# Sums and weighted values of eight heads in one burst: hash-masked attention and a maxout FFN on one core

## The chip, the core and the metric

The kernel runs on one core of one Trainium2 chip. It uses five instruction queues: TensorE (PE, with its weight loads listed as PEld), VectorE (DVE), ScalarE (ACT), GpSimd (POOL) and SyncE (SP, which only issues transfers); POOL and ACT issue transfers too. The metric is the device time of one execution in microseconds (us). Three runs of the kernel before took 264.42, 264.56 and 264.79 us; the median is 264.56 us. The times of the profile were taken on one further execution, of 264.41 us, whose span from the first to the last instruction is 262.4 us.

## The reference: what is computed

Attention over 4 batches, 8 heads, 768 positions and a head size of 64, in which a query sees only keys of the same hash bucket (six sign bits of a projection), and then, over the rows with the heads side by side, a maximum of three products and an output product:

```python
q_bits = (einsum('bhsd,dk->bhsk', q, proj) > 0)      # six bits, likewise k_bits
mask = q_bucket[:, :, :, None] == k_bucket[:, :, None, :]
scores = where(mask, scale * q @ k.T, -1e9)
attn = exp(scores - max); attn = attn / (attn.sum(-1) + 1e-9)
x = (attn @ v)  -> rows of batch and position, columns of head and size: 3072 x 512
out = maximum(maximum(x @ w1, x @ w2), x @ w3) @ w_out     # 512 -> 768 -> 512
```

## The kernel before, in words

The order of all instructions is written out by hand: each engine executes its own instructions in program order, and the program is one loop over 192 **units** (L613). The queries of a batch are cut into **chunks**: batch 0 into three chunks of 256 queries (chunks 0 to 2), batches 1 to 3 into two of 384 each (chunks 3 to 8). A unit is a part of one chunk and one head: 768 scores in each of 128 partitions. The hash bits are appended as six or eight further rows to q and k, so that one matmul gives the masked score.

**A unit.** `scores(u)` (L282) issues two or three PE matmuls (L298) into one of two PSUM buffers `sc`, takes a free SBUF tile `AT` from a list of 24 in order of release, and lets ACT write the exponentials into it (L306). The scores of unit u+1 are issued at the start of turn u. An `AT` tile holds its blocks with two columns of ones behind each; its blocks are 256 or 384 wide, and when a tile is taken in the other width the two columns are written anew, by DVE in `scores` (L304), or by POOL when the tile is given back (L395, for the second half of the heads of batch 0). From chunk 3 on DVE adds the parts of one head together (`add`, L322, two turns behind the unit), and from chunk 5 on also the two halves of that sum.

**A burst** (`burst`, L341) serves one chunk and four heads. It runs one turn behind the last of these heads' units in batch 0, and four turns behind later. Its `sums` is a set of matmuls with 32 columns of ones per head (L358), four heads side by side in one PSUM bank; DVE transposes the bank in blocks of 32 (L365), adds a small constant and takes the reciprocal of one column per block (L367, L368), and spreads it back by a transpose into `rb` (L369). Its `values`, twice, is 24 matmuls with 32 columns each (L380) and one DVE operation into `xT` (L387), which multiplies by `rb`. Then the `AT` tiles of the four heads are given back. Chunks 3 to 8 have their bursts at turns 63, 75, 87, and so on every 12 turns, up to 183 and one after the last turn.

**The FFN** (`ffn_groups`, L402) of a chunk is a list of groups: 18 groups of four matmuls (L413; six column blocks times three weights), whose first product of three is copied from PSUM to `ht` and whose second and third are taken into it by a DVE maximum (L422); then two output groups of three matmuls (L457) for every 128 rows, an ACT copy into a buffer `osb` (L461) and a store from SP (L463). One such group is issued per turn up to turn 47 and 1.15 per turn after that, so that chunk 0's six first products are issued at turns 34 to 39, chunk 1's FFN lasts from turn 55 to 74, chunk 2's to 93, and each later one about 21 turns. The first product is copied by ACT where the chunk is 384 wide (L418) and by DVE in batch 0 (L420).

Sums, values, hash and FFN groups share four PSUM banks, taken and given back in rotation (`bank`, L90).

**Later sets.** q and k of batches 1 to 3 come as "sets" of four heads. They are loaded into `nat` buffers, turned by DVE in four transposes of 32-blocks (L202), narrowed by POOL (L207), and placed by SP transfers into `S` (L212). `quad_hash` (L214) is 16 fp32 matmuls (L221), a DVE comparison into `bits` (L224) and four SP transfers (L232) one turn later. Their turns are written out in the set-up ahead of the loop: the four transposes of a set of batch 2 are spread over nine turns from turn 61 on, of batch 3 over twelve from turn 100 on; a set is placed three turns behind its last transpose; the hash of sets 4, 5, 6 and 7 is issued at turns 84, 99, 135 and 147.

Of the kernel before, what the change touches and what calls it, by code (L numbers as in the profile page):

```python
# [17 lines left out]
def kernel(  # L18
# [31 lines left out]
    RS = 2.0 ** -5  # L50
    SCALE = 0.125 / (RS * RS)
    EPS = 2.0 ** -60
    NAT = 24
    SPREAD = {2: (61, 9), 3: (100, 12)}
    THIRD_ADD = 5
    LAG = (1, 4)
    ATW = 776

    konst = ctx.enter_context(tc.tile_pool(name="konst", bufs=1))
    nat_pool = ctx.enter_context(tc.tile_pool(name="nat", bufs=6))  # L60
    t32_pool = ctx.enter_context(tc.tile_pool(name="t32", bufs=3))
    t16_pool = ctx.enter_context(tc.tile_pool(name="t16", bufs=3))
    s_pool = ctx.enter_context(tc.tile_pool(name="spool", bufs=6))
    b_pool = ctx.enter_context(tc.tile_pool(name="bpool", bufs=2))
    vo_pool = ctx.enter_context(tc.tile_pool(name="vopool", bufs=4))
    small = ctx.enter_context(tc.tile_pool(name="small", bufs=4))
    ad_pool = ctx.enter_context(tc.tile_pool(name="adpool", bufs=5))
    ys_pool = ctx.enter_context(tc.tile_pool(name="yspool", bufs=2))
    rb_pool = ctx.enter_context(tc.tile_pool(name="rbpool", bufs=2))
    x_pool = ctx.enter_context(tc.tile_pool(name="xpool", bufs=3))  # L70
    h_pool = ctx.enter_context(tc.tile_pool(name="hpool", bufs=8))
    o_pool = ctx.enter_context(tc.tile_pool(name="opool", bufs=2))
    sc_ps = ctx.enter_context(tc.tile_pool(name="sc_ps", bufs=2, space=bass.MemoryType.PSUM))
    ms_ps = ctx.enter_context(tc.tile_pool(name="ms_ps", bufs=1, space=bass.MemoryType.PSUM))

# [2 lines left out]
    pj2 = konst.tile([P, Q], FP32, name="pj2")  # L78
    pst = konst.tile([Q, 2, NBITS], FP32, name="pst")
    ones = konst.tile([P, Q], FP16, name="ones")  # L80
    at_tiles = [konst.tile([P, ATW], FP16, name=f"AT{i}", tag=f"AT{i}") for i in range(NAT)]
    warm = h_pool.tile([P, HALF], FP16, tag="ht", name="warm")
    w_sb = [konst.tile([P, NJC, DF], FP16, name=f"w{i}_sb", tag=f"w{i}_sb") for i in range(3)]
# [22 lines left out]
    def s_tile(name):  # L106
        if name not in s_of:
            s_of[name] = s_pool.tile([D + KB, 4, S], BF16, tag="S", name="S")
        return s_of[name]
# [104 lines left out]
    def quad_hash(g):  # L214
        i, bp = bank()
        ts = [t32.pop((side, g)) for side in range(2)]
        for u in range(2):
            for side in range(2):
                for j in range(2):
                    r = 2 * side + j  # L220
                    nc.tensor.matmul(bp[Q * r : Q * (r + 1), 0:HALF], pj[:, u, :],  # L221
                                     ts[side][:, u, j * HALF : (j + 1) * HALF], start=(u == 0), stop=(u == 1))
        bits = b_pool.tile([P, HALF], BF16, tag="bits", name="bits")
        nc.vector.tensor_scalar(out=bits[:], in0=bp[:, 0:HALF], scalar1=0.0, scalar2=0.5,  # L224
                                op0=AluOp.is_gt, op1=AluOp.subtract)
        give(i)

        def send():
            for side in (1, 0):
                for j in range(2):  # L230
                    r = 2 * side + j
                    nc.sync.dma_start(s_of[side, g][D : D + KB, :, j * HALF : (j + 1) * HALF],  # L232
                                      bits[Q * r : Q * (r + 1), :])
        return send

# [105 lines left out]
    def burst(c, i):  # L341
        b, q0, w = chunks[c]
        held = {}
        rb = []

        def own_bank(key):
            if c == NCH - 1 and i == 1 and key != 1:
                return None, sc_ps.tile([P, 2, 512], FP32, tag="sc", name="sc")[:, 0, :]
            return bank()

        def sums(m0, m1):
            if m0 == 0:
                held["s"] = own_bank("s")
            sm = held["s"][1]
            bs = [sum_blocks(c, 4 * i + x) for x in range(4)]
            for m in range(len(bs[0])):
                for x in range(4):
                    nc.tensor.matmul(sm[Q * x : Q * (x + 1), 0:w], ones[:, :], bs[x][m],  # L358
                                     start=(m == 0), stop=(m == len(bs[0]) - 1))
            if m1 == NM:  # L360
                ys = ys_pool.tile([P, HALF], FP32, tag="ys", name="ys")
                rr = small.tile([P, HALF // Q], FP32, tag="rr", name="rr")
                n = w // Q
                rb.append(rb_pool.tile([P, HALF], FP32, tag="rb", name="rb"))
                nc.vector.transpose(ys[:, 0:w], sm[:, 0:w])  # L365
                give(held["s"][0])
                nc.vector.tensor_scalar(out=rr[:, 0:n], in0=ys[:, 0:w:Q], scalar1=EPS * S, scalar2=None, op0=AluOp.add)  # L367
                nc.vector.reciprocal(rr[:, 0:n], rr[:, 0:n])  # L368
                nc.vector.transpose(rb[0][:, 0:w], rr[:, 0:n].unsqueeze(2).to_broadcast((P, n, Q)))  # L369

        def values(side, m0, m1):
            if m0 == 0:
                held[side] = own_bank(side)
            av = held[side][1]
            first = (b, i, side) not in sv_of
            n = w + 1 if first else w
            for m in range(m0, m1):
                cb = block_of(b, m)
                for x in range(4):
                    nc.tensor.matmul(av[Q * x : Q * (x + 1), 0:n], v_at[2 * b + i][:, x, cb * D + side : (cb + 1) * D : 2],  # L380
                                     weights_of(c, 4 * i + x, m)[:, 0:n], start=(m == 0), stop=(m == NM - 1))
            if m1 == NM:
                if first:
                    sv_of[b, i, side] = small.tile([P, 1], FP32, tag=f"sv{side}", name="sv")
                    nc.vector.tensor_scalar(out=sv_of[b, i, side][:], in0=av[:, w : w + 1], scalar1=EPS, scalar2=None,
                                            op0=AluOp.mult)
                nc.vector.scalar_tensor_tensor(out=xt_of(c)[:, 2 * i + side, 0:w], in0=av[:, 0:w],  # L387
                                               scalar=sv_of[b, i, side][:], in1=rb[0][:, 0:w], op0=AluOp.add, op1=AluOp.mult)
                give(held[side][0])
                if side == 1:  # L390
                    for h in range(4 * i, 4 * i + 4):
                        for n in range(parts_of(c)):
                            a = at_of[unit_at[c, h, n]]
                            if b == 0 and i == 1:
                                nc.gpsimd.memset(blocks(at_tiles[a], HALF)[:, :, HALF : HALF + 2], 1.0)  # L395
                                at_form[a] = HALF
                            at_free.append(a)

        return sums, values


    def ffn_groups(c):  # L402
# [6 lines left out]
        for fb, wi in jobs:  # L409
            def go(fb=fb, wi=wi):  # L410
                k_, ps = bank()
                for jc in range(NJC):
                    nc.tensor.matmul(ps[:, 0:w], w_sb[wi][:, jc, fb * P : (fb + 1) * P], xt[:, jc, 0:w],  # L413
                                     start=(jc == 0), stop=(jc == NJC - 1))
                if wi == 0:
                    hts[fb] = h_pool.tile([P, HALF], FP16, tag="ht", name="ht")
                    if w == HALF:
                        nc.scalar.copy(hts[fb][:, 0:w], ps[:, 0:w])  # L418
                    else:
                        nc.vector.tensor_copy(hts[fb][:, 0:w], ps[:, 0:w])  # L420
                else:
                    nc.vector.tensor_tensor(out=hts[fb][:, 0:w], in0=hts[fb][:, 0:w], in1=ps[:, 0:w], op=AluOp.max)  # L422
                give(k_)
            gs.append(go)
# [54 lines left out]
    def when(u, f, *args):  # L479
        at.setdefault(u, []).append(lambda: f(*args))  # L480

    with tc.manual_schedule():
# [10 lines left out]
        load_quad(1, 2, range(4), nc.sync)  # L493
        nc.vector.memset(pj2[:], 0.0)
        nc.vector.memset(ones[:], 1.0)
        for t in at_tiles:
            nc.vector.memset(blocks(t, THIRD)[:, :, THIRD : THIRD + 2], 1.0)
        for hd in range(2):
# [76 lines left out]
        for g in range(2, NQUAD):  # L575
            b2, i2 = divmod(g, 2)
            need = UPB * b2 + 12 * i2
            for n, side in enumerate((1, 0)):
# [7 lines left out]
                for n2, u2 in enumerate(us):  # L586
                    when(u2, turn, name, n2 // 2, n2 % 2)
                    if n2 % 2:
                        when(u2 + 1, narrow, name, n2 // 2)
                when(us[3] + 3, place, name, range(4))  # L590
            hash_at[{2: 32, 3: 47, 4: need - 12}.get(g, need - 9)] = g
            when({2: 36, 3: 46}.get(g, need - 22), load_v, g)

        ffn, credit = [], 0
# [1 line left out]
        last_of = {}  # L596
        for c, i in sorted(done_at, key=lambda e: done_at[e]):
            d = done_at[c, i] + LAG[c > 2]
            sums, values = burst(c, i)
            pieces = [lambda f=sums: f(0, NM), lambda f=values: f(0, 0, NM), lambda f=values: f(1, 0, NM)]  # L600
            for n, f in enumerate(pieces):
                u = {(0, 0): (16, 17, 20), (1, 0): (21, 22, 24), (2, 0): (26, 27, 29)}.get((c, i), (d, d, d))[n]
                todo.setdefault(u, []).append(f)
            last_of[c] = max(u, last_of.get(c, 0))
# [65 lines left out]
```

## Time and profile before

| what | value |
|---|---|
| median of three runs | 264.56 us |
| profiled execution | 264.41 us |
| its span | 262.4 us |
| PE busy | 256.5 us (98%) |
| DVE busy | 207.8 us (79%) |
| ACT busy | 177.9 us (68%) |
| POOL busy | 69.8 us (27%) |
| granted TensorE clock | 1.00 throughout |
| DVE busy from 75 to 111 us | 34.72 of 36 us |
| ACT busy from 60 to 75 us | 12.54 of 15 us |

How to read it: a group of instructions is given by line, engine, operation, tiles and count, then its busy time, the mean duration of one, and the idle time of its engine just before it with what ended that. In the timeline, neighbouring instructions of one kind are merged: start, length from the first start to the last end, engine, line, tiles, count. Matmuls overlap: the next one starts long before the one ahead has ended, and so the distance from start to start tells how long PE is taken, and a duration does not. The same holds to a smaller degree for ACT and DVE, whose next instruction starts up to 0.11 us ahead of the recorded end of the last.

### The profile page before, as it was taken

The numbers are of one execution on the slowest core, as the hardware profiler recorded it, in microseconds if no ns is written. First come the engines' busy times: TensorE is split into PE (matmuls) and PEld (weight loads), VectorE is DVE, ScalarE is ACT, GpSimd is POOL, SyncE is SP. The second block draws the span as 40 slices with busy tenths as digits, with TensorE's granted clock in tenths as the row PEclk, the third lists the DMA queues.
The fourth block names the chain that finished last, engine by engine and source line by source line (L and its number), as shares of the span: only waits on it lengthen the run. The fifth ranks groups of instructions, "written<-read, shape, count | busy, mean of one in ns | idle before, by whom it ended". The sixth has DMA issues, their size and how long they took to land.

```text
span 262.4 us, 6477 instructions
## 1 busy us (share of the span) xinstructions
PE 256.5 (98%) x2503; PEld 154.4 (59%) x2503; DVE 207.8 (79%) x492; ACT 177.9 (68%) x258; POOL 69.8 (27%) x132
## 2 busy tenths in 40 slices
PE   8999999999999999999999999999999999999995
PEld 4655658865765666555555554655555555555552
DVE  2897767966799999969999996899849795888350
ACT  3797886667968675956869588584886859581322
POOL 3878752355043526330141612011000000000000
PEclk9999999999999999999999999999999999999999
DMA  6998999979732964970073653802030003000303
GB/s 210 326 224 170 170 235 226 217 132 204 187 91 75 202 139 61 273 186 17 0 198 104 116 127 49 210 0 58 20 122 1 0 2 121 2 0 2 120 0 120
DMA packets 20717, 30.95 MB, mean 118 GB/s; under 512 B 2608, under 2 KB 15248, under 8 KB 20688
## 3 DMA queue, kind: packets, MB, share of 16 engines
q0 software_dynamic: 8128, 13.37, 27.3%
q1 hardware_dynamic: 12128, 16.66, 22.0%
q10 hardware_dynamic: 432, 0.52, 0.6%
q8 instruction: 19, 0.31, 0.5%
q14 instruction: 10, 0.08, 0.1%
HBM read 25.17 MB, written 6.29 MB: 120 GB/s over the span
## 4 chain that ended last, share of the span: by engine, by line
PE 89%; DVE 5%; ACT 3%; issue 2%; DVEq 0%; ACTq 0%
PE ms L413 34%; PE sc L298 22%; PE ms L457 11%; PE ms L380 10%; PE ms L221 3%; ACT AT L306 3%; PE ms L358 3%; PE ms L171 1%; PE ms L123 1%; PE ms L504 1%; DVE ht L422 1%; DVE ad L329 1%; DVE xT L387 1%; PE ms L150 1%; PE ms L438 1%
## 5 line engine op out<-in xcount | busy, mean ns | idle before, releaser
L306 ACT ACTIVATE AT<-sc 128x768 f16<-128x768 f32 x192 | 152.4, 816 | 57.2 <-PE sc L298 53.9
L413 PE MATMUL ms<-xT,w_sb 128*128 128x384 f16 (+1 forms) x648 | 115.0, 307 | 0.3 <-DVE xT L387 0.2
L298 PE MATMUL sc<-S 72*128 72x384 bf16 (+1 forms) x432 | 93.8, 308 | 1.2 <-ACT AT L306 0.9
L413 PEld LDWEIGHTS <-w_sb 128*128 128x128 f16 x648 | 62.7, 97 | 35.9 <-issue 0.4
L422 DVE TENSOR_TENSOR ht<-ht,ms 128x384 f16<-128x384 f16 (+1 forms) x108 | 54.2, 503 | 20.7 <-PE ms L413 10.5
L298 PEld LDWEIGHTS <-S 72*128 72x128 bf16 (+1 forms) x432 | 39.4, 98 | 31.8 <-issue 11.8
L207 POOL TENSOR_SCALAR T<-T 128x768 bf16<-128x768 f32 x24 | 22.8, 951 | 90.2 <-issue 48.4
L457 PE MATMUL ms<-wout_sb,ht 128*128 128x512 f16 x138 | 35.5, 378 | 0.0
L380 PE MATMUL ms<-AT,vo 128*32 128x385 f16 (+3 forms) x840 | 34.2, 308 | 0.0
L380 PEld LDWEIGHTS <-vo 128*32 128x32 f16 x864 | 22.9, 96 | 9.2 <-issue 1.7
L329 DVE TENSOR_TENSOR ad<-ad,AT 128x768 f16<-128x768 f16 x48 | 26.6, 553 | 2.1 <-ACT AT L306 1.3
L202 DVE STREAM_TRANSPOSE T<-nat 128x384 f32<-128x384 f32 x48 | 26.8, 564 | 0.0
L329 DVE TENSOR_TENSOR ad<-AT,AT 128x768 f16<-128x768 f16 x48 | 26.2, 546 | 0.2 <-ACT AT L306 0.2
L418 ACT CAST ht<-ms 128x384 f16<-128x384 f32 x36 | 17.3, 480 | 8.1 <-PE ms L413 8.1
L457 PEld LDWEIGHTS <-ht 128*128 128x128 f16 x138 | 13.3, 97 | 13.0 <-issue 0.3
L387 DVE SCALAR_TENSOR_TENSOR xT<-ms,sv,rb 128x384 f16<-128x384 f32 (+1 forms) x35 | 19.2, 565 | 1.3
L461 ACT COPY osb<-ms 128x512 f32<-128x512 f32 x21 | 12.2, 586 | 7.5 <-PE ms L457 5.8
L332 DVE TENSOR_TENSOR ad<-ad 128x384 f16<-128x384 f16 x32 | 15.5, 484 | 1.1
L137 POOL TENSOR_SCALAR S<-T 64x384 bf16<-64x384 f32 (+1 forms) x23 | 14.1, 616 | 4.9 <-DVE T L132 3.3
L196 POOL DMA_DIRECT2D nat<-in_q_dram x20 | 11.1, 560 | 0.1
L365 DVE STREAM_TRANSPOSE ys<-ms 128x384 f32<-128x384 f32 (+1 forms) x17 | 9.0, 531 | 2.3 <-PE ms L358 2.0
L176 DVE TENSOR_SCALAR S<-ms 6x384 bf16<-6x384 f32 x16 | 8.9, 554 | 2.0 <-PE ms L171 1.2
(52 smaller groups left out, 122.6 us busy)
## 6 DMA issues: line engine op xcount, KB each, us to landing
out_dram<-osb SPq DMA_DIRECT2D x21, 256.0 KB
S<-T SPq DMA_DIRECT2D x48, 96.0 KB
nat<-in_q_dram POOLq DMA_DIRECT2D x20, 192.0 KB, 6.3
vo<-in_v_dram POOLq DMA_DIRECT2D x8, 384.0 KB, 5.8
nat<-in_k_dram POOLq DMA_DIRECT2D x16, 192.0 KB, 5.7
w_sb<-in_moe_w_dram POOLq DMA_DIRECT2D x3, 768.0 KB, 12.8
nat<-in_k_dram SPq DMA_DIRECT2D x10, 192.0 KB
nat<-in_k_dram SPq DMA_DIRECT2D x3, 384.0 KB
```

What stands on the lines that cost most here:

```text
L202: nc.vector.transpose(t32[name][:, u, half * HALF : (half + 1) * HALF], i_)
L207: nc.gpsimd.tensor_scalar(out=t16[name][:, u, :], in0=t32[name][:, u, :], scalar1=RS, scalar2=1.0, op0=AluOp.mult, op1=AluOp.mult)
L298: nc.tensor.matmul(views[j], s_of[kn][0 : D + bits, kx, m * P : (m + 1) * P], s_of[qn][0 : D + bits, qx, q0 : q0 + w], start=True, stop=True)
L306: nc.scalar.activation(t[:, :, 0:w], whole, ActFn.Exp, bias=-SCALE * 0.25 * bits, scale=SCALE)
L329: nc.vector.tensor_tensor(out=sum_of[c, h][:], in0=t[0], in1=t[n], op=AluOp.add)
L332: nc.vector.tensor_tensor(out=t[:, 0, :], in0=t[:, 0, :], in1=t[:, 1, :], op=AluOp.add)
L380: nc.tensor.matmul(av[Q * x : Q * (x + 1), 0:n], v_at[2 * b + i][:, x, cb * D + side : (cb + 1) * D : 2], weights_of(c, 4 * i + x, m)[:, 0 ...
L387: nc.vector.scalar_tensor_tensor(out=xt_of(c)[:, 2 * i + side, 0:w], in0=av[:, 0:w], scalar=sv_of[b, i, side][:], in1=rb[0][:, 0:w], op0=A ...
L413: nc.tensor.matmul(ps[:, 0:w], w_sb[wi][:, jc, fb * P : (fb + 1) * P], xt[:, jc, 0:w], start=(jc == 0), stop=(jc == NJC - 1))
L418: nc.scalar.copy(hts[fb][:, 0:w], ps[:, 0:w])
L422: nc.vector.tensor_tensor(out=hts[fb][:, 0:w], in0=hts[fb][:, 0:w], in1=ps[:, 0:w], op=AluOp.max)
L457: nc.tensor.matmul(ps[:, 0:DM], hts[fb][:, tb * P : (tb + 1) * P], wout_sb[:, fb, :], start=(fb == 0), stop=(fb == NFB - 1))
```

## The change

Chunks 3 to 7 get one burst for all eight heads, at the turn of the former second one (75, 99, 123, 147, 171). Its sums go into one bank: a new constant `ones2` has ones in 16 of 32 columns, so that rows 0 to 15 of a block hold the sum of one head of the first four and rows 16 to 31 that of one of the second four; one transpose, one addition and one reciprocal then serve eight heads, and `rb` is still spread twice. Batch 0 and chunk 8 keep their bursts of four. `AT` tiles are 29 instead of 24, the sums `ad` nine instead of five. `nat` buffers go from six to four, `t32` from three to two, and `osb` from two to three. The first products of batch 0 are copied by ACT like the others. The transposes for batch 2 begin three turns earlier, later sets (4 to 7) are placed five turns behind their last transpose, and the hashes of sets 4 to 7 are issued at turns 75, 99, 123 and 147, just ahead of the bursts there.

```diff
-    NAT = 24
-    SPREAD = {2: (61, 9), 3: (100, 12)}
+    NAT = 29
+    SPREAD = {2: (58, 9), 3: (100, 12)}
...
-    nat_pool = ctx.enter_context(tc.tile_pool(name="nat", bufs=6))
-    t32_pool = ctx.enter_context(tc.tile_pool(name="t32", bufs=3))
+    nat_pool = ctx.enter_context(tc.tile_pool(name="nat", bufs=4))
+    t32_pool = ctx.enter_context(tc.tile_pool(name="t32", bufs=2))
...
-    ad_pool = ctx.enter_context(tc.tile_pool(name="adpool", bufs=5))
+    ad_pool = ctx.enter_context(tc.tile_pool(name="adpool", bufs=9))
...
-    o_pool = ctx.enter_context(tc.tile_pool(name="opool", bufs=2))
+    o_pool = ctx.enter_context(tc.tile_pool(name="opool", bufs=3))
...
+    ones2 = konst.tile([P, 2, Q], FP16, name="ones2")
...
-                    nc.sync.dma_start(s_of[side, g][D : D + KB, :, j * HALF : (j + 1) * HALF],
+                    nc.sync.dma_start(s_tile((side, g))[D : D + KB, :, j * HALF : (j + 1) * HALF],
...
-        return sums, values
+        return sums, values, rb
+
+    def burst_of_8(c):
+        w = chunks[c][2]
+        n = w // Q
+        _, values0, rb0 = burst(c, 0)
+        _, values1, rb1 = burst(c, 1)
+        k_, sm = bank()
+        bs = [sum_blocks(c, h) for h in range(H)]
+        nb = len(bs[0])
+        for i in range(2):
+            for m in range(nb):
+                for x in range(4):
+                    nc.tensor.matmul(sm[Q * x : Q * (x + 1), 0:w], ones2[:, i, :], bs[4 * i + x][m],
+                                     start=(i == 0 and m == 0), stop=(i == 1 and m == nb - 1))
+        ys = ys_pool.tile([P, HALF], FP32, tag="ys", name="ys")
+        rr = small.tile([P, n, 2], FP32, tag="rr2", name="rr2")
+        rr1 = rr.rearrange("p n i -> p (n i)")
+        nc.vector.transpose(ys[:, 0:w], sm[:, 0:w])
+        give(k_)
+        nc.vector.tensor_scalar(out=rr1, in0=ys[:, 0 : w : Q // 2], scalar1=EPS * S, scalar2=None, op0=AluOp.add)
+        nc.vector.reciprocal(rr1, rr1)
+
+        def spread(i, rb):
+            rb.append(rb_pool.tile([P, HALF], FP32, tag="rb", name="rb"))
+            nc.vector.transpose(rb[0][:, 0:w], rr[:, :, i : i + 1].to_broadcast((P, n, Q)))
+
+        spread(0, rb0)
+        values0(0, 0, NM)
+        spread(1, rb1)
+        values0(1, 0, NM)
+        values1(0, 0, NM)
+        values1(1, 0, NM)
...
-                    if w == HALF:
-                        nc.scalar.copy(hts[fb][:, 0:w], ps[:, 0:w])
-                    else:
-                        nc.vector.tensor_copy(hts[fb][:, 0:w], ps[:, 0:w])
+                    nc.scalar.copy(hts[fb][:, 0:w], ps[:, 0:w])
...
+        nc.vector.memset(ones2[:], 0.0)
+        for i in range(2):
+            nc.vector.memset(ones2[:, i, i * Q // 2 : (i + 1) * Q // 2], 1.0)
...
-                when(us[3] + 3, place, name, range(4))
-            hash_at[{2: 32, 3: 47, 4: need - 12}.get(g, need - 9)] = g
+                when(us[3] + (3 if g < 4 else 5), place, name, range(4))
+            hash_at[{2: 32, 3: 47, 4: 75, 5: 99, 6: 123, 7: 147}[g]] = g
...
-            sums, values = burst(c, i)
+            if 2 < c < NCH - 1:
+                if i == 1:
+                    todo.setdefault(d, []).append(lambda c=c: burst_of_8(c))
+                    last_of[c] = d
+                continue
+            sums, values, _ = burst(c, i)
```

## The prediction

> **What bounds the kernel now.** I read the busy shares first, then the list of waits, then PE's timeline, and at last ACT's and DVE's timelines where the change puts work.
>
> ```profile
> PE 256.5 (98%) x2503; PEld 154.4 (59%) x2503; DVE 207.8 (79%) x492; ACT 177.9 (68%) x258; POOL 69.8 (27%) x132
> ...
> PE sc L298 <- ACT AT L306: 0.9, 3, 0.3
> ...
> PE ms L413 <- DVE xT L387: 0.2, 1, 0.2
> ```
>
> PE sets the time, and the list of waits has only a microsecond of it waiting for others. But durations of matmuls overlap, so I read starts. This is PE's timeline around the burst of turn 87 and the hash of turn 84:
>
> ```profile
> 95.84 0.60 PE L413 MATMUL ms<-xT,w_sb 128*128 128x256 f16 x4
> 96.37 1.50 PE L221 MATMUL ms<-T,pj 128*32 128x384 f32 x16
> 97.80 0.50 PE L298 MATMUL sc<-S 72*128 72x384 bf16 x2
> 98.14 0.60 PE L413 MATMUL ms<-xT,w_sb 128*128 128x256 f16 x4
> 98.57 0.49 PE L298 MATMUL sc<-S 72*128 72x384 bf16 x2
> 98.90 0.60 PE L413 MATMUL ms<-xT,w_sb 128*128 128x256 f16 x4
> 99.34 0.49 PE L298 MATMUL sc<-S 72*128 72x384 bf16 x2
> 99.67 0.60 PE L413 MATMUL ms<-xT,w_sb 128*128 128x256 f16 x4
> 100.20 0.51 PE L358 MATMUL ms<-ad,ones 128*32 128x384 f16 x8
> 100.53 2.12 PE L380 MATMUL ms<-AT,vo 128*32 128x384 f16 x48
> 102.59 0.50 PE L298 MATMUL sc<-S 72*128 72x384 bf16 x2
> ```
>
> An FFN group ahead of scores takes 0.43 us from start to start (98.14 to 98.57), ahead of sums or hash 0.53 (99.67 to 100.20, 95.84 to 96.37): 0.09 to 0.10 goes by where PE changes from 128 columns of weights to 32. On the way back it is the same: 48 value matmuls are 12 fours of 0.163 (half of the 0.33 of the eight sums), 1.95 us, and took 2.06 (100.53 to 102.59): 0.11 more. The hash is four fours, which start 0.32 apart in the trace, and takes 1.43: 0.12 more on its way out. Elsewhere after turn 50 the starts lie as close as the widths allow, but for 0.30 us at 80.9 us and 0.07 at 139.8. So whatever is put on PE, or in its way, is paid in full.
>
> ACT, at turns 36 to 41, then with copies of an FFN product between exponentials, three exponentials back to back, and the prices of copies:
>
> ```profile
> 41.91 5.32 ACT L306 ACTIVATE AT<-sc 128x768 f16<-128x768 f32 x7 [3.03 <-PE sc L298]
> ...
> 112.31 0.47 ACT L418 CAST ht<-ms 128x384 f16<-128x384 f32 x1
> 112.67 1.71 ACT L306 ACTIVATE AT<-sc 128x768 f16<-128x768 f32 x2
> ...
> 138.91 2.24 ACT L306 ACTIVATE AT<-sc 128x768 f16<-128x768 f32 x3
> ...
> L418 ACT CAST ht<-ms 128x384 f16<-128x384 f32 x36 | 17.3, 480 | 8.1 <-PE ms L413 8.1
> ...
> L442 ACT COPY nat<-ms 128x256 f32<-128x256 f32 x1 | 0.4, 372 | 0.1
> ```
>
> An exponential takes ACT 0.705 us from start to start when it need not wait ((2.24 - 0.83) / 2). A turn of batch 0's FFN takes PE 0.767 (0.33 scores, 0.43 group). ACT has 0.06 us to spare per turn there. A score matmul of turn u+2 waits for the exponential of u; by the trace's rows that exponential ends only 0.13 us before, and where the wait binds 0.05, so the slack is 0.08.
>
> **The change part by part.** The sum is made against the profiled execution (264.41 us, span 262.4, so 2.0 around it), 0.15 below the median of 264.56.
>
> *Bursts of eight.* The number of matmuls is the same: `ones2` doubles the sums' fours in one burst and there is one burst less. Of bursts 63, 87, 111, 135 and 159 only the two changes of width go: 0.09 + 0.11 each, 1.00 in all. The lone hash of turn 84 now stands right ahead of burst 75 and shares its changes (0.21). The hash of 135 was beside a burst and is again; those of 99 and 147 stay. Together **-1.21 us**. Bounds: nothing (the changes are paid another way), and -1.3.
>
> The Trainium skill (TensorE: Matmul & The Clock Gate, section "Step-by-step: what each phase is for") says that PE pulls the next weights into the array while earlier matmuls still run, out of a window of 64 instructions. By that alone a change of width would cost nothing, the sum would lack this part and be 266.0 us; all rows above show the gap.
>
> *DVE in these bursts* loses five transposes (0.53), additions (0.17) and reciprocals (0.22), 4.6 us, and batch 0's 18 copies (0.41), 7.4 us. DVE is beside PE; what this gives is the stall at 80.9 us, where PE waited for a bank that DVE had not read: **-0.30**. The stall at 139.8 us came from ACT waiting for an `osb` buffer; the third buffer takes it: **-0.07**.
>
> *Copies on ACT.* In place: the 384-wide one takes 0.36 (112.31 to 112.67); a column is (480 - 372) / 128 = 0.84 ns, so a 256-wide one takes 0.25. Bounds 0.20 and its full 0.37. Six come in a row at turns 34 to 39: ACT then needs 0.705 + 0.25 = 0.955 per turn against PE's 0.767, 0.19 too much. Four of them lie ahead of a score matmul before burst 40 (turn 41 waits for exponential 39, behind copies 34 to 37); the last two vanish behind the burst, where ACT idled over 2 us. 4 x 0.19 less 0.08 and a little at the start: **+0.66**. In chunk 1 and 2 one turn in three has a copy: the two others win back the slack of 0.08, the third loses 0.19, 0.11 net, more right behind chunk 0's output copies; where a turn has two groups nothing is lost. Counting by the turns of front: chunk 1 +0.43, chunk 2 +0.35. Burst 63 and 87, which let ACT catch up, are gone, and are counted. Together **+1.44**; with 0.20 per copy 0.9, with 0.37 1.9 to 2.3.
>
> *29 AT tiles.* Five tiles of batch 0 now meet chunk 3 in the old width, by the order of the list at units 48 to 52, and get their ones from DVE (L304), not from POOL. The exponential waits for this: those of units 48 on wait for POOL's semaphore now. At unit 50 it costs:
>
> ```profile
> 60.08 3.11 ACT L306 ACTIVATE AT<-sc 128x768 f16<-128x768 f32 x4 [2.15 <-POOL AT L395]
> ...
> 59.76 0.88 DVE L387 SCALAR_TENSOR_TENSOR xT<-ms,sv,rb 128x256 f16<-128x256 f32 x2
> 60.55 0.41 DVE L422 TENSOR_TENSOR ht<-ht,ms 128x256 f16<-128x256 f16 x1
> ```
>
> The memset stands in DVE's queue behind both `xT` operations of burst 48, which end at 60.64; it takes 0.06. The exponential starts at 60.7 rather than 60.08, and the score matmul of unit 52 behind it is late by that less 0.08: **+0.53**. Bounds 0 and 0.65. The other four hide: 48 and 49 ahead of burst 48, 51 and 52 behind unit 50's delay. Queued behind them on DVE is only the maximum of the next group, whose bank PE needs three groups later.
>
> *The longer burst.* PE is 4.2 us on it without giving ACT work; ACT idles longer, at no cost, as PE is behind it after that. From chunk 3's FFN on a turn is 0.98 of PE against 0.705 + 0.12 of ACT. DVE has `ys` to `rb` (0.53 + 0.17 + 0.22 + 0.53), four `xT` (0.53 apart) and one more spread (0.5): 4.1 us, beside 4.2 of PE. The next FFN group takes the bank of the first `xT`, which is read 2 us earlier. Nothing, if DVE is not 2 us behind; `ys` started at most 0.81 us behind its sums in the trace.
>
> *Queues and buffers.* Set 2's four SP loads now wait for the first `nat` buffer (PE's transposes, 8.4 us) instead of being issued at 5.9; their first reader runs at 30.2, and SP has nothing else until 22.5: nothing. `t32` with two: the third set's copy at 16.2 us finds POOL done at 10.4, the fourth's at some 21 us at 15.8. Three new memsets at the start lie in DVE's 2.6 us of waiting for `proj`. Placing at +5 leaves set 7's second half six turns less one before unit 156; four transfers took SP 3.6 us (179.05 on) and have 5: nothing. The hash at 75 is two turns behind its last transpose, as that of 147 was, without a stall.
>
> Sum: -1.21 - 0.30 - 0.07 + 1.44 + 0.53 = **+0.39**, 264.41 to 264.8 us.
>
> **The rivals.**
> 1. *ACT's additions are hidden.* If a copy costs at most the slack (0.06 per turn, 0.08 once) or the exponentials close up behind it, the +1.44 goes: 264.8 - 1.44 = 263.4, faster. For it: ACT is only 84% busy from 60 to 75 us. Against: starts at 0.767 with no idle time between. It decides from copies below 0.1 us.
> 2. *Copies at their full duration*, 0.37: +2.3 instead of 1.44 and 0.6 for the memset: 265.8, slower. Against: 0.36 for the wider one.
> 3. *DVE late behind the longer burst*: the first FFN group after each waits. With a backlog of 2.4 us (three times the 0.81 seen) 0.4 per burst, five of them: 264.8 + 2.0 = 266.8. For it: DVE is 96% busy from 75 to 111 us. Against: it loses 12 us.
> 4. *Fewer changes of width bring nothing*, so that the first part doesn't do what it says: 264.8 + 1.2 = 266.0. All rows speak against it. It is what the Trainium skill's rule above would give.
>
> **How the numbers follow.** A difference under 0.2% (0.53 us) can't be told from no change here. My forecast, with its own range of 264.0 to 265.4, has 0.50: 0.36 of it within 0.2% of the median (264.03 to 265.09), 0.12 above, 0.02 below. Rival 1 has 0.26, rival 2 0.13, rival 3 0.07, rival 4 0.04. Faster 0.28, same 0.36, slower 0.36. The range reaches from 263.2 (rival 1, with the copies' lower price in the rest) to 266.2 (rivals 2 and 4).
>
> **What would show it.** PE: seven bursts instead of twelve from chunk 3 on, five of them with 96 value matmuls in some 4.0 us and one pair of gaps. ACT: starts 0.95 apart at turns 35 to 40, score matmuls of turns 39 to 41 late by 0.2 to 0.65; an exponential that waits for DVE's L304 after burst 48. No PE stall at 80.9 us. PE's first group after a burst without wait. It is wrong if PE's starts in batch 0's FFN stay at 0.767, or if PE waits for a bank behind a burst.

## The result, and the profile after

The changed kernel takes 265.27 us (median of 16 runs, 264.67 to 266.14) against 264.53 us of the kernel before (16 runs, 263.98 to 265.54). The ratio is 1.0026, with a 95% interval of 1.0014 to 1.0038: slower by 0.4 to 1.0 us. The prediction had +0.39 us and a range of 263.2 to 266.2. The profiled execution took 264.99 us, with a span of 262.8 us.

The page's busy times and the list of waits of the changed kernel, in the lines that answer to those shown of before:

```profile
PE 256.1 (97%) x2503; PEld 155.8 (59%) x2503; DVE 199.2 (76%) x472; ACT 180.7 (69%) x276; POOL 69.9 (27%) x132
...
PE sc L299 <- ACT AT L307: 1.3, 4, 0.5
...
PE ms L447 <- DVE xT L388: 0.2, 1, 0.2
```

DVE is busy for 8.6 us less, ACT for 2.8 more, and PE has the same number of matmuls. The list of waits shows little, as before, because overlapping durations hide short waits. PE's timeline at turns 75 and 76 shows a burst of eight (start, length, engine, line, tiles, count):

```profile
84.90 0.60 PE L447 MATMUL ms<-xT,w_sb 128*128 128x256 f16 x4
85.43 1.50 PE L222 MATMUL ms<-T,pj 128*32 128x384 f32 x16
86.75 0.83 PE L414 MATMUL ms<-ad,ones 128*32 128x384 f16 x16
87.40 4.13 PE L381 MATMUL ms<-AT,vo 128*32 128x385 f16 x96
91.46 0.50 PE L299 MATMUL sc<-S 72*128 72x384 bf16 x2
```

The FFN group takes 0.53 to the next start: one change of width, 0.09 more than 0.43. From hash to sums (1.32 for four fours 0.32 apart) and from sums to values (0.65 for four fours of 0.163) nothing is lost. The 24 fours of values take 4.06, 0.15 more than 24 x 0.163: 0.04 of it is the extra column of these matmuls (385 instead of 384; on 48 of them it costs 0.02, 2.08 us for the burst of turn 75 against 2.06 for that of 87 in the kernel before), the other 0.11 the second change. One pair of gaps where there were three: burst 63, burst 75 and the hash of 84 had one each.

What a change of width does is seen in the weight loads (PEld). These rows are of the kernel before, ahead of burst 87, and of the changed kernel, behind burst 75:

```profile
99.51 0.48 PEld L413 LDWEIGHTS <-w_sb 128*128 128x128 f16 x4
100.20 0.12 PEld L358 LDWEIGHTS <-ones 128*32 128x32 f16 x8 [0.21 <-issue]
...
91.46 0.11 PEld L299 LDWEIGHTS <-S 72*128 72x128 bf16 x2 [0.32 <-issue]
```

The FFN group's first load starts at 99.51, 0.16 ahead of its first matmul (99.67), while the matmul before that runs. The first load of the sums starts only at 100.20, with their first matmul, and so does the load of the scores behind the burst (91.46). In both traces it is so at every change of width after 41 us, 33 in the kernel before and 21 in the changed one: the load starts at most 5 ns ahead of its matmul. Between two matmuls with 128 columns of weights it is at least 0.10 us ahead. Twelve changes less for 1.18 us is 0.10 for each.

To tell where the time went I added up, for every kernel, what PE's starts lie apart beyond their widths, from turn 34 on, by what ended the gap (gaps over 20 ns; worked out from the single starts in the trace). The last two columns are the times of whole executions, and "34 to 191" runs from the first score matmul of unit 34 to that of unit 191, so that the start of the kernel, which differed by up to 1.7 us from one profiled execution to another, is left out.

| kernel | changes of width | ACT | DVE | 34 to 191, us | median, us | against before |
|---|---|---|---|---|---|---|
| before | 3.23 | 0.07 | 0.65 | 193.68 | 264.53 | |
| changed | 2.05 | 2.16 | 0.35 | 194.15 | 265.27 | 1.0026 [1.0014, 1.0038] |
| e1, all copies back on DVE | 2.05 | 0.59 | 2.49 | 194.75 | 265.80 | 1.0044 [1.0030, 1.0058] |
| e2, ones early | 2.06 | 1.74 | 0.16 | 193.54 | 264.69 | 1.0003 [0.9993, 1.0012] |
| e3, both | 2.06 | 0.02 | 1.79 | 193.84 | 265.09 | 1.0020 [1.0010, 1.0030] |
| e4, bursts of eight split | 3.05 | 2.86 | 0.35 | 195.89 | 267.19 | 1.0096 [1.0080, 1.0111] |
| e5, before, copies on ACT | 3.22 | 1.16 | 0.50 | 194.72 | 265.46 | 1.0035 [1.0024, 1.0046] |
| e6, ones early, chunk 0 on DVE | 2.05 | 0.78 | 0.35 | 192.75 | 263.86 | 0.9977 [0.9965, 0.9989] |
| e7, e3 with later transposes | 2.25 | 0.00 | 0.47 | 192.39 | 263.39 | 0.9950 [0.9934, 0.9965] |
| e8, before, earlier transposes | 3.10 | 0.29 | 2.57 | 195.86 | 266.73 | 1.0085 [1.0064, 1.0105] |

The kernel before ran again beside the experiments, at 264.59 us (e1 to e4) and 264.56 us (e5 to e8). The change in "34 to 191" and the change in the median against these runs agree within 0.4 us in each row.

The changed kernel thus gave up 1.18 us of changes of width and 0.30 of DVE, and took on 2.09 us of ACT. The ACT part is seen in two places. First, ACT at turns 34 to 36, in ACT's timeline:

```profile
43.23 0.38 ACT L451 CAST ht<-ms 128x256 f16<-128x256 f32 x1
43.48 0.84 ACT L307 ACTIVATE AT<-sc 128x768 f16<-128x768 f32 x1
44.19 0.41 ACT L451 CAST ht<-ms 128x256 f16<-128x256 f32 x1
44.44 0.87 ACT L307 ACTIVATE AT<-sc 128x768 f16<-128x768 f32 x1
45.14 0.43 ACT L451 CAST ht<-ms 128x256 f16<-128x256 f32 x1
45.39 0.90 ACT L307 ACTIVATE AT<-sc 128x768 f16<-128x768 f32 x1
```

and the score matmuls in PE's timeline of the same turns:

```profile
43.46 0.49 PE L299 MATMUL sc<-S 70*128 70x256 bf16 x3
...
44.38 0.49 PE L299 MATMUL sc<-S 70*128 70x256 bf16 x3
...
45.36 0.49 PE L299 MATMUL sc<-S 70*128 70x256 bf16 x3
...
46.34 0.49 PE L299 MATMUL sc<-S 70*128 70x256 bf16 x3
```

In the kernel before they were:

```profile
43.59 0.49 PE L298 MATMUL sc<-S 70*128 70x256 bf16 x3
...
44.36 0.49 PE L298 MATMUL sc<-S 70*128 70x256 bf16 x3
...
45.13 0.49 PE L298 MATMUL sc<-S 70*128 70x256 bf16 x3
```

A copy takes 0.25 from start to start (43.23 to 43.48), an exponential 0.71, 0.95 to 0.96 together; the score matmuls follow at 0.98 where they had 0.77. The 0.98 is the distance of the exponentials' recorded ends: these are 44.32, 45.31 and 46.29 (start plus length), as the length grows by 0.03 from one to the next, and each time the score matmul that takes the emptied buffer starts some 0.05 behind the end (44.38, 45.36, 46.34).

Second, DVE, ACT and PE behind burst 48:

```profile
60.41 0.88 DVE L388 SCALAR_TENSOR_TENSOR xT<-ms,sv,rb 128x256 f16<-128x256 f32 x2
...
61.24 0.40 DVE L305 MEMSET AT<- 128x4 f16 x2
...
61.43 3.02 ACT L307 ACTIVATE AT<-sc 128x768 f16<-128x768 f32 x4 [2.61 <-PE sc L299]
...
60.13 0.50 PE L299 MATMUL sc<-S 72*128 72x384 bf16 x2
...
60.91 0.49 PE L299 MATMUL sc<-S 72*128 72x384 bf16 x2
61.24 0.60 PE L447 MATMUL ms<-xT,w_sb 128*128 128x256 f16 x4
62.29 0.48 PE L299 MATMUL sc<-S 72*128 72x384 bf16 x2 [0.45 <-ACT AT L307]
```

The exponential of unit 50, whose scores were issued at 60.13, starts only at 61.43, right behind the memset, which stood behind both `xT` (the row merges the memsets of units 50 and 51; one takes 0.06). The timeline names the score matmul as its releaser, but that one had been done for 0.8 us. Two turns on, PE waits: 61.24 to 62.29 is 1.05 for a group of 0.43, 0.62 lost.

### The profile page after: what moved, and what is told of

Read it like the earlier page. It is cut to its first block, busy times and chain, and to the rows that moved or that the text cites. A ratio compares the mean times of both kernels' runs of the same rounds, so it can differ in the third digit from the quotient of the medians.

```text
span 262.8 us, 6491 instructions
## 1 busy us (share of the span) xinstructions
PE 256.1 (97%) x2503; PEld 155.8 (59%) x2503; DVE 199.2 (76%) x472; ACT 180.7 (69%) x276; POOL 69.9 (27%) x132
## 4 chain that ended last, share of the span: by engine, by line
PE 90%; ACT 7%; issue 1%; DVE 0%; ACTq 0%
PE ms L447 34%; PE sc L299 23%; PE ms L381 11%; PE ms L488 11%; ACT AT L307 5%; PE ms L222 3%; PE ms L359 2%; PE ms L124 1%; PE ms L538 1%; PE ms L172 1%; PE ms L414 1%; ACT ht L451 1%; PE ms L151 1%; PE ms L469 1%; PE sc L381 0%
## 5 line engine op out<-in xcount | busy, mean ns | idle before, releaser
L381 PE MATMUL ms<-AT,vo 128*32 128x385 f16 (+3 forms) x840 | 33.4, 308 | 0.0
L451 ACT CAST ht<-ms 128x384 f16<-128x384 f32 (+1 forms) x54 | 24.5, 454 | 8.8 <-PE ms L447 8.8
L381 PEld LDWEIGHTS <-vo 128*32 128x32 f16 x864 | 23.6, 96 | 8.5 <-issue 1.3
L330 DVE TENSOR_TENSOR ad<-AT,AT 128x768 f16<-128x768 f16 x48 | 27.7, 578 | 0.2 <-ACT AT L307 0.2
L197 POOL DMA_DIRECT2D nat<-in_k_dram x16 | 9.0, 570 | 0.4
```

Source lines behind the costliest of these rows:

```text
L197: eng.dma_start(dst, src)
L330: nc.vector.tensor_tensor(out=sum_of[c, h][:], in0=t[0], in1=t[n], op=AluOp.add)
```

## The experiments

**The copies back on DVE (e1).** The edit:

```diff
-                    nc.scalar.copy(hts[fb][:, 0:w], ps[:, 0:w])
+                    if w == HALF:
+                        nc.scalar.copy(hts[fb][:, 0:w], ps[:, 0:w])
+                    else:
+                        nc.vector.tensor_copy(hts[fb][:, 0:w], ps[:, 0:w])
```

> The changed kernel with the first products of batch 0 copied by VectorE again, all else kept. Theory (ScalarE pays): the late score matmuls of turns 38 to 41 (0.78 us in the changed kernel's trace), of turns 59 to 67 (0.47) and 81 to 88 (0.27) go, 1.5 us; VectorE may give back up to the 0.3 us that it cost before. Span 262.8 - 1.5 + 0 to 0.3 = 261.3 to 261.6, 1.2 to 1.5 us faster than the changed kernel and 0.8 to 1.1 faster than the one before. Rival (VectorE needs the relief: bursts of eight bunch its work, and it was 96% busy from 75 to 111 us): stalls for VectorE come back in that stretch and eat the 1.5 us, span 262.8 or more.

My theory fell, and the rival's outcome came: 265.80 us, 0.5 us slower than the changed kernel. ACT's part went as expected (2.16 to 0.59; what is left is the memset), but DVE's grew from 0.35 to 2.49, all of the growth in turns 68 to 73 and 86 to 91 (the gaps there sum to 0.90 and 1.25). PE's timeline of this kernel at turns 88 to 90:

```profile
101.13 0.60 PE L447 MATMUL ms<-xT,w_sb 128*128 128x256 f16 x4
102.19 0.60 PE L447 MATMUL ms<-xT,w_sb 128*128 128x256 f16 x4 [0.46 <-DVE ht L454]
102.62 0.49 PE L299 MATMUL sc<-S 72*128 72x384 bf16 x2
102.95 0.60 PE L447 MATMUL ms<-xT,w_sb 128*128 128x256 f16 x4
103.39 0.49 PE L299 MATMUL sc<-S 72*128 72x384 bf16 x2
103.97 0.81 PE L491 MATMUL ms<-wout_sb,ht 128*128 128x512 f16 x3
```

and DVE's there:

```profile
99.99 0.55 DVE L330 TENSOR_TENSOR ad<-AT,AT 128x768 f16<-128x768 f16 x1
100.46 0.41 DVE L456 TENSOR_TENSOR ht<-ht,ms 128x256 f16<-128x256 f16 x1
100.79 0.57 DVE L203 STREAM_TRANSPOSE T<-nat 128x384 f32<-128x384 f32 x1
101.28 0.52 DVE L330 TENSOR_TENSOR ad<-ad,AT 128x768 f16<-128x768 f16 x1
101.72 0.41 DVE L454 CAST ht<-ms 128x256 f16<-128x256 f32 x1
102.24 0.42 DVE L456 TENSOR_TENSOR ht<-ht,ms 128x256 f16<-128x256 f16 x1
```

The second group of the turn waits 0.62 (101.13 to 102.19, less 0.43) for a PSUM bank that a DVE copy has not yet read; DVE goes from one operation to the next. So in the changed kernel the copies on ACT had been paid for by something: 1.5 us of ACT kept off 2.1 us of DVE. But DVE had these copies in the kernel before too, with 4.6 us of burst work more, and lost PE only 0.30 there. What made it late was open: the bursts of eight, as the rival says, or the transposes that start three turns earlier. That is what e7 and e8 are for.

**The ones early (e2).** Added in the set-up, beside `fill_pj`:

```diff
+        def refit():
+            for a in at_free[2:7]:
+                if at_form[a] != HALF:
+                    nc.gpsimd.memset(blocks(at_tiles[a], HALF)[:, :, HALF : HALF + 2], 1.0)
+                    at_form[a] = HALF
+        when(44, refit)
```

> The changed kernel, but the five AT tiles that meet chunk 3 in the old width get their ones at turn 44 from GpSimd instead of at turns 47 to 51 from VectorE. Theory (the exponential of unit 50 waits behind VectorE's xT): the stall of 0.62 us of the score matmul of turn 52 goes, span 262.2, the rest of the trace unchanged. Rival (that exponential is late for another reason, as ScalarE's lag after the longer row of copies): the stall stays, span 262.8.

264.69 us, 0.58 faster than the changed kernel; from 34 to 191 it is 0.61. The theory held: no score matmul waits at turn 52. (The table's ACT column falls by only 0.42, because the wait at turn 34, 0.35 under DVE in the changed kernel, shows here as 0.16 under DVE and 0.19 under ACT.) The span of its profile, 262.9, does not show it: 0.45 us more went by between the last matmul (259.30 against 259.64) and the end, and the start was later by 0.26. ACT's line behind burst 48 has the exponential of unit 50 start 0.62 behind its first score matmul (60.40), where it was 0.59 in the kernel before and 1.30 in the changed one:

```profile
61.02 3.09 ACT L307 ACTIVATE AT<-sc 128x768 f16<-128x768 f32 x4 [2.15 <-POOL AT L396]
```

**Both together (e3).** The two edits above in one kernel.

> Copies back on VectorE and the ones early, together. Theory: the two are separate, 262.8 - 1.5 - 0.6 + 0 to 0.3 = 260.7 to 261.0 us of span, some 1.5 us faster than the kernel before. Rival (VectorE needs the relief): 262.2 or more.

265.09 us, 0.5 slower than the kernel before, where the theory had 1.5 faster. The ones early were worth about what they were alone (0.7 against e1), and 1.79 us of DVE's stalls stayed, 0.35 of it the wait at turn 34 that the kernel before has too, with a gap of 0.37 at 68.7 us for which the trace names no releaser. The rival's outcome again.

**The bursts of eight split (e4).** In `burst_of_8`:

```diff
         values0(1, 0, NM)
+        nonlocal credit
+        credit -= 1
+        ffn.pop(0)()
         values1(0, 0, NM)
```

> The changed kernel, with one FFN group of 128 columns of weights moved from the next turn into the middle of each of the five bursts of eight, so that five pairs of changes of width come back and nothing else is added. Theory (a change of width costs 0.09 and 0.11 us): five times 0.20, span 263.8. Rival (the gain of the longer burst has another cause, as VectorE's shorter chain): span 262.8, within 0.2.

267.19 us, 1.9 more than the changed kernel, about twice what was expected. PE's timeline at burst 75:

```profile
87.84 2.16 PE L381 MATMUL ms<-AT,vo 128*32 128x385 f16 x48
89.93 0.61 PE L450 MATMUL ms<-xT,w_sb 128*128 128x256 f16 x4
90.47 2.16 PE L381 MATMUL ms<-AT,vo 128*32 128x385 f16 x48
92.56 0.82 PE L299 MATMUL sc<-S 72*128 72x384 bf16 x4
```

The group takes 0.54 instead of 0.43, and the values ahead of it 2.09 instead of 1.97. Changes of width rose by 1.00 us, 0.20 for each pair: this is what the theory named. Another 0.70 us came from ACT: the turn behind the burst has lost its FFN group, so that four score matmuls stand together (92.56, x4), and PE reaches the next ones before ACT has emptied a buffer. That is a side effect of this edit, and no part of the change.

**The copies on ACT in the kernel before (e5).** The copy of L420 made by ACT, all else as before.

> The kernel before, with the one edit that batch 0's first products are copied by ScalarE. Theory (a copy on ScalarE delays PE where turns are 0.767 us): +0.7 us at turns 38 to 41 as in the changed kernel, +0.2 to 0.4 in chunks 1 and 2, where bursts 63 and 87 let ScalarE catch up, and -0.3 for the VectorE stall at 80.9 us: last matmul 0.6 to 0.8 us later than in the kernel before. Rival (these copies cost only in company with the bursts of eight): no later than 0.2 us.

265.46 us, 0.9 slower than before; from 34 to 191 it is 1.04, more than the 0.6 to 0.8 expected. ACT rose by 1.09: 0.74 at units 38 to 41 and 0.42 at units 59, 62 and 81, while the 0.07 for the `osb` buffer went. DVE fell by 0.15 alone: the stall at 80.9 us went, but one of 0.15 at 133 us came. A further 0.14 goes by inside the last values of burst 111, at 135 us, and the trace names nothing that it waited for. So the copies have their price on ACT with bursts of four as well.

**Chunk 0's copies on DVE, those of chunks 1 and 2 on ACT, ones early (e6).** The changed kernel with the edit of e2 and, in place of the edit of e1:

```diff
-                    nc.scalar.copy(hts[fb][:, 0:w], ps[:, 0:w])
+                    if c > 0:
+                        nc.scalar.copy(hts[fb][:, 0:w], ps[:, 0:w])
+                    else:
+                        nc.vector.tensor_copy(hts[fb][:, 0:w], ps[:, 0:w])
```

> The changed kernel with the ones early, chunk 0's six copies back on VectorE and those of chunks 1 and 2 left on ScalarE. Theory (ScalarE is short of time in turns 34 to 41, VectorE in turns 66 to 91, each where the other is not): -0.78 and -0.61 against the changed kernel and no VectorE stall, last matmul 1.4 us earlier than in the changed kernel and 1.0 earlier than in the one before, about 263.5 to 263.9 us. Rival (any copy taken back by VectorE leaves it late further on): last matmul within 0.4 us of that of the kernel before.

263.86 us, a ratio of 0.9977 [0.9965, 0.9989], faster than both kernels. From 34 to 191 it is 1.40 less than the changed kernel and 0.93 less than the one before. At turns 34 to 41 DVE takes the copies at no cost.

**Later transposes (e7).** The kernel of e3 with

```diff
-    SPREAD = {2: (58, 9), 3: (100, 12)}
+    SPREAD = {2: (61, 9), 3: (100, 12)}
...
-            hash_at[{2: 32, 3: 47, 4: 75, 5: 99, 6: 123, 7: 147}[g]] = g
+            hash_at[{2: 32, 3: 47, 4: 78, 5: 99, 6: 123, 7: 147}[g]] = g
```

> Copies all on VectorE and the ones early, as in the third run, but batch 2's transposes begin at turn 61 again, as in the kernel before, and the hash of set 4 follows at turn 78, between two FFN groups. Theory A (VectorE's stalls of 1.2 us before the bursts of 75 and 99 come from the transposes, which at 58 fall on FFN turns and at 61 in part on the output turns 71 to 74 and 90 to 93, where VectorE has no maximum): the stalls fall to 0.3 us or less, one pair of changes of width comes back (+0.21): last matmul 0.7 us earlier than in the third run. Theory B (they come from bunching: without bursts 63 and 87 PE makes VectorE's work faster than VectorE does it): stalls stay at 1 us or more, last matmul 0.2 later than in the third run.

263.39 us, the fastest of all: 0.9950 [0.9934, 0.9965] of the kernel before. Theory A held. DVE's stalls fell from 1.79 to 0.47 us, of which 0.35 is the wait for `xT` at turn 34; changes of width rose by 0.19. The same PE stretch as in e1, turns 88 to 91:

```profile
100.47 1.04 PE L447 MATMUL ms<-xT,w_sb 128*128 128x256 f16 x8
101.34 0.49 PE L299 MATMUL sc<-S 72*128 72x384 bf16 x2
101.67 0.60 PE L447 MATMUL ms<-xT,w_sb 128*128 128x256 f16 x4
102.11 0.49 PE L299 MATMUL sc<-S 72*128 72x384 bf16 x2
102.44 0.81 PE L491 MATMUL ms<-wout_sb,ht 128*128 128x512 f16 x3
103.08 0.49 PE L299 MATMUL sc<-S 72*128 72x384 bf16 x2
```

Eight matmuls of two groups run through (100.47 to 101.34, 0.87) where e1 had 0.62 us between them. This kernel has the bursts of eight without the parts of the change that cost time, the copies on ACT, the late ones and the early transposes: it is 1.2 us faster than the kernel before, 0.98 of that in changes of width.

**Earlier transposes in the kernel before (e8).** `SPREAD` from 58 and the hash of set 4 at 75, nothing else.

> The kernel before with batch 2's transposes from turn 58 on and the hash of set 4 at turn 75, beside burst 75, copies on VectorE and bursts of four as they were. Theory A (transposes): PE stalls for VectorE by some 1 us in turns 66 to 91, less 0.21 for the shared change of width: last matmul 0.5 us or more later. Theory B (bunching): no more stall than the 0.30 there is, last matmul 0.2 us earlier.

266.73 us, 2.2 slower than before, with bursts of four and all. DVE's stalls rose from 0.65 to 2.57 us, in turns 66 to 91 again, the one at burst 87 in the sums themselves, which waited for DVE's additions:

```profile
PE ms L358 <- DVE ad L329: 0.6, 1, 0.6
```

Theory A again, in a second kernel; bunching alone (theory B) is out, as e7 has the bursts of eight without the stalls, and e8 the stalls without the bursts of eight. Both runs move more than the transposes: the loads and the narrowing go with them, and the hash of set 4, with its comparison on DVE, was moved as well. The hash can't be the cause of all of it: of e8's stalls 0.94 us lie in turns 68 to 73, ahead of the hash, and the stalls are gone with the hash at turn 78 (e7) as they are small with it at 84 (before). That output turns, which give DVE no maximum, are what takes up the later transposes fits with where the stalls lie, but no run moved the transposes turn by turn, and I leave that part as argued.

## Why the prediction was right, point by point

- *Bursts of eight*, -1.21: measured -1.18 (3.23 to 2.05), and confirmed by putting five pairs back (0.20 each). In these traces all but a few bursts lose 0.09 going in and 0.10 to 0.12 coming out, and the weight loads start with their matmuls there, so the Trainium skill's rule weighed in the prediction (TensorE: Matmul & The Clock Gate, section "Step-by-step: what each phase is for") doesn't reach to a change of width. Rival 4 is out.
- *DVE in these bursts*, -0.30 and -0.07: both stalls are gone. What took them is not what the term says: e5, with bursts of four and two `osb` buffers, loses both as well, so the copies are enough for the first, and no run shows that the third buffer is what took the second. DVE's busy time fell by 8.6 us, where the forecast had 12.0; among others, the recorded lengths of the 48 first additions of two tiles grew by 1.5 us in sum. And the reason was incomplete. I wrote that DVE is beside PE, so that the 7.4 us of copies taken off it could give no more than the stall that was there. The trace of before showed DVE 96% busy from 75 to 111 us, and the same change moved batch 2's transposes to an earlier place within this stretch. I gave that move no price at all. By e8 it costs 1.9 us of DVE stalls in the kernel before, and by e3 against e7 1.3 us with the bursts of eight, when the copies are on DVE (the hash of set 4 moves along in both); the copies on ACT kept it off. This part of the forecast was luck. The sum came out because a cost that I had not seen was covered by a relief that I had priced at almost nothing.
- *Copies on ACT*, +1.44: measured 0.80 (units 38 to 41; I had 0.66), 0.48 in chunk 1 (0.43) and 0.27 in chunk 2 (0.35), 1.55 together. The price of one in place, 0.25, worked out from the wider copy and two rows, is what the trace has. What was small is the price of a turn: I took it from the starts, 0.955, 0.19 too much, but PE waits for the recorded ends, which lie 0.98 apart, and the score matmuls of units 39 to 41 each come 0.22 late. The errors in chunk 1 (0.05 too little) and chunk 2 (0.08 too much) partly cancel. Rival 1 (hidden) and rival 2 (full duration, 0.37) are out.
- *29 AT tiles*, +0.53: measured 0.62, and e2 takes it away. It was a wait of ACT on DVE, 0.06 us of work behind 0.88 of another.
- *The longer burst*: no wait for a bank behind any of the five bursts in the changed kernel. Rival 3 is out as it was put (behind the bursts); DVE's lateness was real, but lay in turns 68 to 73, ahead of the first burst of eight, and 86 to 91, 11 turns and more behind it.
- *Queues and buffers* at nothing: no new wait there in the changed kernel.

By these terms the sum is -1.18 - 0.30 - 0.07 + 1.55 + 0.62 = +0.62 us; from 34 to 191 it is +0.47, the profiled executions differ by 0.58 and the medians by 0.74 (0.37 to 1.0 by the interval). The predicted +0.39 was at the lower end; the ACT terms were 0.2 us small in all. The measured time also lies above the band of 264.03 to 265.09 us, in which the forecast had put 0.36 of its 0.50.

## What to carry to other kernels

When one engine is bound and two others are each nearly full in some stretch, a copy moved from one to the other is priced in both, turn by turn: here ACT was short in turns 34 to 41 (0.705 us of each 0.767) and DVE in 68 to 91 (96% busy from 75 to 111 us), and with the early transposes the best place differed between them (e6). Every line of a diff that shifts work in time needs a price of its own, even where it moves no work from one engine to another: starting batch 2's transposes three turns earlier, with the hash that goes with them, cost 1.9 us of stalls in the kernel before, more than the 1.2 us that the longer bursts gained. And a small instruction on a busy queue costs what stands ahead of it, if a bound engine waits for it two steps later.

## What the runs showed of the hardware that was not expected

On ACT, the recorded duration grows along a run of back-to-back work while the starts stay evenly apart: exponentials of 0.84, 0.87, 0.90 us and copies of 0.38, 0.41, 0.43 us at turns 34 to 37 of the changed kernel, with starts 0.71 and 0.25 apart throughout, so that the next start comes to lie up to 0.26 us ahead of the recorded end (0.18 in the kernel before, where the 0.11 given at the outset is too small). The starts tell how long ACT is taken. But what waits for ACT's result waits for the recorded end: the late score matmuls of units 38 to 41 start 0.05 us behind it, in the changed kernel and in e5 alike, so PE is released every 0.98 us where ACT itself needs 0.955. And profiled executions of these kernels, which hardly differ up to turn 33, reached unit 34 between 41.1 and 42.8 us, and needed 3.1 to 3.6 us from the last matmul to the end, so that spans of single profiles differ by more than the effects looked for here.
